# Threshold attention and a three-way max FFN: from two stages over DRAM to one fused, software-pipelined loop

## The chip, the cores and the metric

The kernel runs on one core of one Trainium2 chip. The metric is the device time of one execution, in microseconds; of several runs the median is taken.

## The reference

Sizes: 8 batches, 8 heads, 576 tokens, head width 64; q, k and v are fp32. The FFN has d_model 512 and d_ff 768 over 4608 tokens.

```python
scores = (q @ k.T) / sqrt(64)
thresh = max(scores, axis=-1) - tau                   # tau = 0.02
scores = where(scores >= thresh, scores, -1e9)
attn = exp(scores - max(scores)); attn = attn / (sum(attn) + 1e-9)
x = (attn @ v) laid out as 4608 x 512                 # heads side by side
h = maximum(maximum(x @ w1, x @ w2), x @ w3)          # 4608 x 768
out = h @ w_out                                       # fp32
```

Whether a score is kept depends on a difference of 0.02 from its row's maximum, and both kernels compute the scores in fp32; P, V, x and the weights are bf16.

## The kernel before

There are two stages, with x between them in DRAM (`xT`, 512 x 4608, bf16).

Attention loops over 64 heads. A head's 576 tokens are cut into five chunks, four of 128 and one of 64. For each chunk SyncE's queue loads v, q and k (lines 74 to 77, 32 KB each), VectorE casts v to bf16 (line 75), TensorE transposes q and k in one fp32 transpose (line 79) and VectorE copies the two halves out (lines 80, 81), both to partitions 0 to 63. Then, for each of five query chunks, two fp32 matmuls over 512 and 64 keys (line 89) with ScalarE copying the scaled scores out of PSUM (line 91), the row maximum and its negative on VectorE (lines 95, 97), Exp on ScalarE (line 99), one VectorE instruction that compares e with exp(-tau), multiplies, and sums the row (line 102), the reciprocal (108), and the division to bf16 `eall` (109). Last, for each key chunk, five bf16 transposes of P on TensorE (line 118), each copied out of PSUM by VectorE (line 120), and two matmuls with V as the stationary operand (lines 121, 124), accumulating the transposed output over key chunks; five casts and five stores to `xT` end the head (lines 130, 131).

The score tiles and the q/k transposes share a PSUM tag of two buffers ("sc"); the transposes of P have two of their own ("tr").

The FFN first loads the four weights (1536 KB each, fp32) and casts them on VectorE (lines 142, 147). Then 36 tiles of 128 tokens: a load of x, 24 matmuls of 384 columns (line 163, x stationary), a running maximum on VectorE (lines 167, 169), a cast (172), six transposes of h with copies (176, 177), six matmuls of 512 columns (180), a copy (183) and a store (184).

Waits and buffers are placed by the framework from the tiles' dependences, and it also orders each engine's instructions ahead of time, not strictly by the program: in the trace the next head's transposes of line 79 stand between this head's transposes of line 118. Within an engine the order is then fixed. Each DMA is issued by the engine named in the call: all of them by SyncE (SP in the profile).

## Time and profile before

| | before |
|---|---|
| runs | 2002.81, 2003.24, 2004.69 us; median 2003.24 |
| span of the profiled execution | 2002.6 us, its own time as far as it is recorded; 0.6 below the median |
| TensorE matmuls / weight loads | 80% / 36% of the span |
| VectorE, ScalarE | 67%, 23% |
| granted TensorE clock | 1.00 of full speed in every slice |
| DMA engines | q1 10.8% of 16 engines' span |

A share of busy time is an average over the two stages. The durations of TensorE instructions contain their latency, so what one more of a kind costs is read from the distance of starts, or from merged rows ("x7") that give the time of several in sequence. Idle time is put down to the instruction that ended last before the wait was over.

### The profile page before, as it was taken

The page shows a single profiled execution, that of the slowest core. Times are in us where ns is not written, and L with a number is a line of the kernel's source. Part 1 is how long each engine was busy: PE and PEld are TensorE (multiplying, and loading weights), DVE is VectorE, ACT ScalarE, POOL GpSimd, SP SyncE. Part 2 cuts the span into 40 slices and gives each one's busy share as a digit, 9 for nine tenths or more (in the row PEclk, how much of TensorE's full clock was granted, in tenths as well). Part 3 has the DMA queues.
Part 4 walks back from the last instruction along what each step waited for, and adds up shares of the span by engine and source line. Part 5 has one row for each costly group of instructions (what it writes and reads, how often), then busy time and mean ns, then how long its engine had stood idle before and what let it go on. Part 6 is the DMA issues. An engine that isn't in the chain of part 4 may idle for free.

```text
span 2002.6 us, 20193 instructions
## 1 busy us (share of the span) xinstructions
PE 1596.6 (80%) x5136; PEld 714.2 (36%) x5136; DVE 1349.6 (67%) x5308; ACT 461.1 (23%) x961; POOL 1.5 (0%) x10
## 2 busy tenths in 40 slices
PE   6777778877777877777787777788777778589998
PEld 3333333333333333333333333333333333244544
DVE  5666666666666666666666666666666666577777
ACT  2222222222222222222222222222222222100000
POOL 0000000000000000000000000000000000000000
PEclk9999999999999999999999999999999999999999
DMA  1000100000000000000000000000000000131121
GB/s 23 21 21 20 26 20 18 21 21 21 19 19 21 17 21 21 21 19 19 20 18 21 21 21 18 20 18 20 21 21 20 19 21 18 35 141 61 59 64 53
DMA packets 178227, 54.85 MB, mean 27 GB/s; under 512 B 171200, under 2 KB 171200, under 8 KB 178112
## 3 DMA queue, kind: packets, MB, share of 16 engines
q1 hardware_dynamic: 178112, 53.56, 10.8%
q8 instruction: 42, 0.69, 0.1%
q14 instruction: 73, 0.60, 0.1%
HBM read 39.32 MB, written 14.16 MB: 27 GB/s over the span
## 4 chain that ended last, share of the span: by engine, by line
PE 58%; DVE 26%; ACT 9%; issue 5%; DMA 1%; SPq 0%; ACTq 0%; DVEq 0%
PE ptile L89 28%; PE at L118 10%; DVE e L102 9%; PE optile L121 9%; ACT e L99 5%; DVE ats L120 5%; DVE mx L95 4%; ACT scores L91 4%; PE pt L163 4%; PE tp L79 3%; DVE eall L109 3%; PE op L180 3%; DVE hmax L169 2%; PE optile L124 2%; DVE hb L172 1%
## 5 line engine op out<-in xcount | busy, mean ns | idle before, releaser
L89 PE MATMUL ptile<-kT,qT 64*128 64x512 f32 (+3 forms) x1280 | 771.6, 746 | 70.0 <-ACT scores L91 69.9
L118 PE MATMUL at<-identb,eall 128*128 128x128 bf16 (+3 forms) x1600 | 371.9, 277 | 191.1 <-DVE ats L120 153.6
L91 ACT ACTIVATE scores<-ptile 128x512 f32<-128x512 f32 (+3 forms) x640 | 246.2, 405 | 1148.4 <-PE ptile L89 1148.0
L89 PEld LDWEIGHTS ptile<-kT,qT 64*128 64x128 f32 (+1 forms) x1280 | 341.4, 302 | 424.3 <-issue 206.7
L120 DVE COPY ats<-at 128x128 bf16<-128x128 bf16 (+3 forms) x1600 | 302.9, 211 | 252.9 <-PE at L118 224.2
L102 DVE SCALAR_TENSOR_TENSOR e<-e 128x576 f32<-128x576 f32 (+1 forms) x320 | 239.4, 748 | 281.5 <-ACT e L99 272.3
L118 PEld LDWEIGHTS <-eall 128*128 128x128 bf16 (+3 forms) x1600 | 164.9, 118 | 548.2 <-DVE eall L109 274.4
L99 ACT ACTIVATE e<-scores,nmx 128x576 f32<-128x576 f32 (+1 forms) x320 | 246.4, 771 | 120.7 <-DVE nmx L97 120.6
L95 DVE TENSOR_REDUCE mx<-scores 128x1 f32<-128x576 f32 (+1 forms) x320 | 237.8, 743 | 20.5 <-ACT scores L91 20.5
L121 PE MATMUL optile<-ats,vS 128*64 128x512 bf16 (+1 forms) x320 | 194.9, 609 | 68.6 <-DVE ats L120 68.0
L163 PE MATMUL pt<-t,xt 128*128 128x384 bf16 x864 | 178.8, 331 | 31.8 <-DVE t L142 18.0
L109 DVE TENSOR_SCALAR eall<-e,rs 128x576 bf16<-128x576 f32 (+1 forms) x320 | 161.9, 506 | 0.0
L79 PE MATMUL tp<-identf,vf 128*128 128x128 f32 (+1 forms) x320 | 123.4, 427 | 34.4 <-ACT scores L91 19.4
L163 PEld LDWEIGHTS <-xt 128*128 128x128 bf16 x864 | 85.2, 99 | 109.4 <-issue 56.9
L169 DVE TENSOR_TENSOR hmax<-hmax,pt 128x384 f32<-128x384 f32 x144 | 76.4, 551 | 34.8 <-PE pt L163 34.3
L81 DVE COPY kT<-tp 64x128 f32<-64x128 f32 (+1 forms) x320 | 89.4, 279 | 8.7
L80 DVE COPY qT<-tp 64x128 f32<-64x128 f32 (+1 forms) x320 | 84.2, 263 | 11.3 <-PE tp L79 4.3
L79 PEld LDWEIGHTS tp<-identf,vf 128*128 128x128 f32 (+1 forms) x320 | 56.4, 191 | 70.0 <-ACT scores L91 31.0
L124 PE MATMUL optile<-ats,vS 128*64 128x64 bf16 (+1 forms) x320 | 76.9, 240 | 3.7
L130 DVE CAST osb<-optile 64x128 bf16<-64x128 f32 (+1 forms) x320 | 73.4, 259 | 3.5 <-DMA xT<-osb 3.1
L121 PEld LDWEIGHTS <-vS 128*64 128x64 bf16 (+1 forms) x320 | 41.8, 131 | 64.7 <-issue 53.1
L180 PE MATMUL op<-wo,hT 128*128 128x512 bf16 x216 | 64.6, 381 | 0.0
(25 smaller groups left out, 413.0 us busy)
## 6 DMA issues: line engine op xcount, KB each, us to landing
out_dram<-osb SPq DMA_DIRECT2D x36, 256.0 KB, 2.0
vf<-in_v_dram SPq DMA_DIRECT2D x256, 32.0 KB, 1.7
vf<-in_q_dram SPq DMA_DIRECT2D x256, 32.0 KB, 1.8
vf<-in_k_dram SPq DMA_DIRECT2D x256, 32.0 KB, 1.8
xt<-xT SPq DMA_DIRECT2D x36, 128.0 KB, 2.2
tf<-in_moe_w_dram SPq DMA_DIRECT2D x3, 1536.0 KB, 9.8
xT<-osb SPq DMA_DIRECT2D x256, 16.0 KB, 1.7
wof<-in_moe_w_out_dram SPq DMA_DIRECT2D x1, 1536.0 KB, 16.7
```

Of the source, the lines that this page charges most:

```text
L79: nc.tensor.transpose(tp[:, :ck], vf[:ck, 1:].rearrange("p a d -> p (a d)"), identf[:ck, :ck])
L89: nc.tensor.matmul(ptile[:pm, :nn], qT[:, mo:mo + pm], kT[:, n0:n0 + nn], start=True, stop=True)
L91: nc.scalar.activation(out=scores[:pm, n0:n0 + nn], in_=ptile[:pm, :nn], func=Copy, scale=scale)
L95: nc.vector.reduce_max(mx[:pm], scores[:pm], axis=AX)
L99: nc.scalar.activation(out=e[:pm], in_=scores[:pm], func=Exp, bias=nmx[:pm], scale=1.0)
L102: nc.vector.scalar_tensor_tensor(out=e[:pm], in0=e[:pm], scalar=thr, in1=e[:pm], op0=AluOpType.is_ge, op1=AluOpType.mult, accum_out=sm[:pm])
L109: nc.vector.tensor_scalar_mul(eall[:pm, m], e[:pm], rs[:pm])
L118: nc.tensor.transpose(at[:ck, :pm], eall[:pm, m, co:co + ck], identb[:pm, :pm])
L120: nc.vector.tensor_copy(out=ats[:ck, m, :pm], in_=at[:ck, :pm])
L121: nc.tensor.matmul(optile[:, :4, :].rearrange("p a b -> p (a b)"), vS[:ck, c, :], ats[:ck, :4, :].rearrange("p a b -> p (a b)"), start=(c ...
L163: nc.tensor.matmul(pt, xt[:, kc, :], wt[:, kc, nb*384:nb*384+384], start=(kc == 0), stop=(kc == 3))
L180: nc.tensor.matmul(op, hT[:, c, :], wo[:, c, :], start=(c == 0), stop=(c == 5))
```

## The change

Nearly the whole body is replaced. What it does:

- One loop over 32 pairs of heads (four pairs a batch); the FFN of a batch is cut into 18 pieces (one that transposes X, 12 of hidden units, 5 of output rows), and one piece is put behind each unit of the attention of the next batch.
- q and k are loaded twice or in halves so that, after the fp32 transposes, q stands on partitions 0 to 63 and again on 64 to 127, and the first 288 keys on partitions 0 to 63, the other 288 on 64 to 127. A score tile is two matmuls of 288 columns, one on each half of the rows of the array, into two PSUM banks (`scores`).
- A pair has five units: units 0 to 3 take 128 queries of both heads, unit 4 the last 64 of both. The maximum is taken from PSUM directly. In units 0 to 2 ScalarE applies Prelu with slope 1e30 to score - max + tau: a score below the threshold becomes hugely negative, and the Exp that follows over both heads (1152 columns) makes it zero; no compare on VectorE. Units 3 and 4 take Exp and then the compare-and-multiply on VectorE.
- P is transposed by DMA transposes on SyncE's queue, one a unit, instead of on TensorE. P is padded with zeros to 640 keys.
- V has a 65th column of ones, so that the product with P also gives the row sums; P times V has P's transpose as stationary operand and 65 columns, and only its output is divided.
- The normalized output stays in SBUF (`X`), is transposed by DMA transposes, and the FFN computes h transposed, with the weights as stationary operand; there is no transpose of h, and ScalarE takes the first of the three products and the output copy.
- Weights and V are cast while they are loaded, by DMAs of GpSimd's queue, and the output is stored from that queue.
- P times V runs two units behind its P (`drain(2)`).

The diff, cut to its core; of the removed lines, which are all of the loops described above, four stand for the rest:

```diff
--- before
+++ after
...
-                for (n0, nn) in ((0, 512), (512, 64)):
...
-                nc.vector.tensor_scalar_mul(eall[:pm, m], e[:pm], rs[:pm])
...
-                    nc.tensor.transpose(at[:ck, :pm], eall[:pm, m, co:co + ck],
...
-            nc.tensor.transpose(pt, hb[:, c * 128:(c + 1) * 128], ident)
...
+STEEP = -1.0e30
...
+    wts = []
+    for i, w in enumerate((moe_w1, moe_w2, moe_w3)):
+        t = one.tile([128, 4, DF], BF16, name=f"w{i}")
+        for ko in range(4):
+            nc.gpsimd.dma_start(out=t[:, ko, :], in_=w[ko * 128:(ko + 1) * 128, :])
+        wts.append(t)
+    wo = one.tile([128, 6, DM], BF16, name="wo")
+    for ko in range(6):
+        nc.gpsimd.dma_start(out=wo[:, ko, :], in_=moe_w_out[ko * 128:(ko + 1) * 128, :])
+    NPB = 4
+    p_ring = [one.tile([128, 2, KP], BF16, name=f"pring{i}") for i in range(NPB)]
+    for t in p_ring:
+        nc.vector.memset(t[:, :, S:], 0.0)
+    NVB = 3
+    v_ring = [one.tile([128, 2, NK, D + 1], BF16, name=f"vring{i}") for i in range(NVB)]
...
+    ps_s = ctx.enter_context(tc.tile_pool(name="ps_s", bufs=2, space=PSUM))
+    ps_o = ctx.enter_context(tc.tile_pool(name="ps_o", bufs=1, space=PSUM))
+    ps_f = ctx.enter_context(tc.tile_pool(name="ps_f", bufs=2, space=PSUM))
+    def load(b, hp):
+        h0 = 2 * hp
+        qm = ld.tile([128, 2, 4, 2, D], F32, name="qm")
+        ql = ld.tile([128, 2, D], F32, name="ql")
+        kk = ld.tile([128, 2, 2, 2, D], F32, name="kk")
+        kl = ld.tile([32, 2, 2, D], F32, name="kl")
+        vt = v_ring[(b * NP + hp) % NVB]
+        for i in range(2):
+            h = h0 + i
+            for j in range(2):
+                nc.sync.dma_start(out=qm[:, i, :, j, :],
+                                  in_=q[b, h, 0:512, :].rearrange("(c p) d -> p c d", p=128))
+                nc.sync.dma_start(out=ql[i * 64:(i + 1) * 64, j, :], in_=q[b, h, 512:S, :])
                 nc.sync.dma_start(
+                    out=kk[:, i, :, j, :],
+                    in_=k[b, h, j * HS:j * HS + 256, :].rearrange("(c p) d -> p c d", p=128))
+            nc.sync.dma_start(
+                out=kl[:, i],
+                in_=k[b, h].rearrange("(j u) d -> u j d", j=2)[256:HS])
+            nc.gpsimd.dma_start(out=vt[:, i, 0:4, 0:D], in_=v[b, h, 0:512, :].rearrange("(c p) d -> p c d", p=128))
+            nc.gpsimd.dma_start(out=vt[0:64, i, 4, 0:D], in_=v[b, h, 512:S, :])
+        return dict(b=b, hp=hp, qm=qm, ql=ql, kk=kk, kl=kl, vt=vt)
+    def prep(L):
+        qt = qk.tile([128, 2, 512], F32, name="qt")
+        qtl = qk.tile([128, 128], F32, name="qtl")
+        kt = qk.tile([128, 2, HS], F32, name="kt")
+        for i in range(2):
+            tp = ps_f.tile([128, 512], F32, name="tp", tag="f")
+            for c in range(4):
+                nc.tensor.transpose(
+                    tp[:, c * 128:(c + 1) * 128],
+                    L["qm"][:, i, c].rearrange("p t d -> p (t d)"),
+                    identf)
+            nc.scalar.activation(out=qt[:, i], in_=tp, func=AF.Copy, scale=scale)
+            tk = ps_f.tile([128, 512], F32, name="tk", tag="f")
+            for c in range(2):
+                nc.tensor.transpose(tk[:, c * 128:(c + 1) * 128],
+                                    L["kk"][:, i, c].rearrange("p j d -> p (j d)"), identf)
+            nc.tensor.transpose(tk[:, 256:HS], L["kl"][:, i].rearrange("p j d -> p (j d)"), identf[:32, :32])
+            if i == 1:
+                nc.tensor.transpose(tk[:, 384:512], L["ql"].rearrange("p t d -> p (t d)"), identf)
+                nc.vector.tensor_scalar(out=qtl, in0=tk[:, 384:512], scalar1=scale, scalar2=None, op0=OP.mult)
+            nc.vector.tensor_copy(out=kt[:, i], in_=tk[:, :HS])
+        L.update(qt=qt, qtl=qtl, kt=kt)
+    def scores(L, i, c):
+        ps = ps_s.tile([128, 2, 512], F32, name="ps")
+        if c < 4:
+            for j in range(2):
+                r = slice(j * 64, (j + 1) * 64)
+                nc.tensor.matmul(ps[:, j, :HS], L["qt"][r, i, c * 128:(c + 1) * 128],
+                                 L["kt"][r, i, :], start=True, stop=True)
+        else:
+            for g in range(2):
+                for j in range(2):
+                    r = slice(j * 64, (j + 1) * 64)
+                    nc.tensor.matmul(ps[g * 64:(g + 1) * 64, j, :HS], L["qtl"][r, g * 64:(g + 1) * 64],
+                                     L["kt"][r, g, :], start=True, stop=True)
+        return ps
+    state = {"u": 0}
+    def unit(L, c):
+        n = 2 if c < 4 else 1
+        P = p_ring[state["u"] % NPB]
+        state["u"] += 1
+        masked = c >= 3
+        z = zz.tile([128, 2, S], F32, name="z")
+        for i in range(n):
+            ps = scores(L, i, c)
+            pv = ps[:, :, :HS]
+            nm = small.tile([128, 1], F32, name="nm")
+            nc.vector.tensor_reduce(out=nm, in_=pv, axis=mybir.AxisListType.XY, op=OP.max, negate=True)
+            zi = z[:, i].rearrange("p (j u) -> p j u", j=2)
+            if masked:
+                nc.scalar.activation(out=zi, in_=pv, func=AF.Exp, bias=nm)
+                nc.vector.scalar_tensor_tensor(out=P[:, i, :S], in0=z[:, i], scalar=thr, in1=z[:, i],
+                                               op0=OP.is_ge, op1=OP.mult)
+            else:
+                bm = small.tile([128, 1], F32, name="bm")
+                nc.vector.tensor_scalar_add(bm, nm, tau)
+                nc.scalar.activation(out=zi, in_=pv, func=AF.Prelu, bias=bm, alpha=-STEEP)
+        if not masked:
+            nc.scalar.activation(out=P[:, 0:n, :S], in_=z[:, 0:n], func=AF.Exp)
+        pt = pt_pool.tile([128, 2 * NK, 128], BF16, name="pt")
+        nc.sync.dma_start_transpose(out=pt[:, 0:n * NK, :], in_=P[:, 0:n].rearrange("p h k -> p (h k)"))
+        return pt
+    def pv_unit(L, c, pt):
+        if c == 0:
+            L["o"] = [ps_o.tile([128, 512], F32, name=f"o{i}") for i in range(2)]
+        for i in range(2):
+            o = L["o"][i] if c < 4 else L["o"][1]
+            if c < 4:
+                dst = o[:, c * 65:c * 65 + 65]
+                blk, cols = i * NK, slice(0, 128)
+            else:
+                dst = o[i * 64:(i + 1) * 64, 260:325]
+                blk, cols = 0, slice(i * 64, (i + 1) * 64)
+            for m in range(NK):
+                kr = 128 if m < 4 else 64
+                nc.tensor.matmul(dst, pt[:kr, blk + m, cols], L["vt"][:kr, i, m, :],
+                                 start=(m == 0), stop=(m == NK - 1))
+    def normalize(L, X):
...
+            nc.vector.reciprocal(rs[:, :n], ov[:, :, 64])
+            nc.vector.tensor_tensor(
+                out=X[:, 0:4, h * D:(h + 1) * D], in0=ov[:, 0:4, 0:64],
+                in1=rs[:, 0:4].unsqueeze(2).to_broadcast([128, 4, 64]), op=OP.mult)
...
+    def x_transposed(X):
+        xt = xp.tile([128, 5, 4, 128], BF16, name="xt")
+        for c in range(5):
+            r = 128 if c < 4 else 64
+            nc.sync.dma_start_transpose(out=xt[:, c, :, :r], in_=X[:r, c, :])
+        return xt
...
+        def hid(f, a):
+            c0, c1, r = (0, 2, 128) if a == 0 else (2, 5, 128)
+            hm = hp_.tile([128, 320], BF16, name="hm", bufs=3)
+            n = 256 if a == 0 else 320
+            dst = st["hT"][:, f, 0:256] if a == 0 else st["hT"][:, f, 256:S]
+            for wi in range(3):
+                pt = ps_f.tile([128, 512], F32, name="ph", tag="f")
                 for kc in range(4):
+                    w = wts[wi][:, kc, f * 128:(f + 1) * 128]
+                    if a == 0:
+                        nc.tensor.matmul(pt[:, 0:256], w, st["xt"][:, 0:2, kc, :], start=(kc == 0), stop=(kc == 3))
+                    else:
+                        nc.tensor.matmul(pt[:, 0:256], w, st["xt"][:, 2:4, kc, :], start=(kc == 0), stop=(kc == 3),
+                                         skip_group_check=True)
+                        nc.tensor.matmul(pt[:, 256:320], w, st["xt"][:, 4, kc, :64], start=False,
+                                         stop=(kc == 3), skip_group_check=True)
                 if wi == 0:
+                    nc.scalar.activation(out=hm[:, :n], in_=pt[:, :n], func=AF.Copy)
+                elif wi == 1:
+                    nc.vector.tensor_tensor(out=hm[:, :n], in0=pt[:, :n], in1=hm[:, :n], op=OP.max)
                 else:
+                    nc.vector.tensor_tensor(out=dst, in0=pt[:, :n], in1=hm[:, :n], op=OP.max)
+        for f in range(6):
+            for a in range(2):
+                pieces.append(lambda f=f, a=a: hid(f, a))
+        def outp(c):
+            r = 128 if c < 4 else 64
+            po = ps_f.tile([128, 512], F32, name="po", tag="f")
+            for f in range(6):
+                nc.tensor.matmul(po[:r, :], st["hT"][:, f, c * 128:c * 128 + r], wo[:, f, :],
+                                 start=(f == 0), stop=(f == 5))
+            ob = hp_.tile([128, DM], F32, name="ob", bufs=3)
+            nc.scalar.activation(out=ob[:r], in_=po[:r], func=AF.Copy)
+            nc.gpsimd.dma_start(out=out[b * S + c * 128:b * S + c * 128 + r, :], in_=ob[:r])
+        for c in range(5):
+            pieces.append(lambda c=c: outp(c))
+        return pieces
+    todo = []
+    pairs = [(b, hp) for b in range(B) for hp in range(NP)]
+    L = load(*pairs[0])
+    prep(L)
+    waiting = []
+    X = None
+    def drain(keep):
+        while len(waiting) > keep:
+            Lw, c, pt, Xw = waiting.pop(0)
+            pv_unit(Lw, c, pt)
+            if c == 4:
+                normalize(Lw, Xw)
+                if Lw["hp"] == NP - 1:
+                    todo.extend(ffn_pieces(Lw["b"], Xw))
+    for n, (b, hp) in enumerate(pairs):
+        if hp == 0:
+            X = xp.tile([128, 5, DM], BF16, name="X")
+        Ln = load(*pairs[n + 1]) if n + 1 < len(pairs) else None
+        for c in range(5):
+            pt = unit(L, c)
+            waiting.append((L, c, pt, X))
+            drain(2)
+            if todo:
+                todo.pop(0)()
+            if c == 2 and Ln is not None:
+                prep(Ln)
+        L = Ln
+    drain(0)
+    while todo:
+        todo.pop(0)()
```

## Rows read from the trace of the kernel before

**Rows 1.** The page: busy time and share of each engine, and the granted clock.

```profile
PE 1596.6 (80%) x5136; PEld 714.2 (36%) x5136; DVE 1349.6 (67%) x5308; ACT 461.1 (23%) x961; POOL 1.5 (0%) x10
...
PEclk9999999999999999999999999999999999999999
```

**Rows 2.** Busy time by stretch: one head, and most of the FFN.

```profile
core 0: us, PE busy (x) PEld busy (x) DVE busy (x) ACT busy (x) POOL busy (x), PEclk, DMA share, GB/s
1000.00:1027.05 27.05, 21.46 (x61) 9.31 (x60) 18.15 (x76) 7.19 (x16) 0.00 (x0) 1.00 0.09 19
...
1760.00:2002.60 242.60, 220.25 (x1287) 116.37 (x1284) 183.38 (x504) 0.00 (x0) 0.00 (x0) 1.00 0.21 65
```

**Rows 3.** The page: the chain that ended last, by engine and by line.

```profile
PE 58%; DVE 26%; ACT 9%; issue 5%; DMA 1%; SPq 0%; ACTq 0%; DVEq 0%
PE ptile L89 28%; PE at L118 10%; DVE e L102 9%; PE optile L121 9%; ACT e L99 5%; DVE ats L120 5%; DVE mx L95 4%; ACT scores L91 4%; PE pt L163 4%; PE tp L79 3%; DVE eall L109 3%; PE op L180 3%; DVE hmax L169 2%; PE optile L124 2%; DVE hb L172 1%
```

**Rows 4.** Timeline (start, duration, ..., idle before): the same ScalarE instruction, 26 heads apart.

```profile
1011.58 0.60 ACT L91 ACTIVATE scores<-ptile 128x512 f32<-128x512 f32 x1 [11.06 <-PE ptile L89]
...
1714.81 0.60 ACT L91 ACTIVATE scores<-ptile 128x512 f32<-128x512 f32 x1 [11.06 <-PE ptile L89]
```

**Rows 5.** Timeline of weight loads in the scores of one query chunk.

```profile
1015.86 0.50 PEld L89 LDWEIGHTS ptile<-kT,qT 64*128 64x128 f32 x2 [0.55 <-ACT scores L91]
1016.88 0.33 PEld L89 LDWEIGHTS ptile<-kT,qT 64*128 64x128 f32 x1 [0.52 <-ACT scores L91]
1017.73 0.34 PEld L89 LDWEIGHTS ptile<-kT,qT 64*128 64x128 f32 x1 [0.52 <-issue]
```

**Rows 6.** Timeline of TensorE: instructions of one kind in sequence.

```profile
1024.08 0.69 PE L79 MATMUL tp<-identf,vf 128*128 128x128 f32 x2 [0.30 <-ACT scores L91]
...
1901.83 1.13 PEld L163 LDWEIGHTS <-xt 128*128 128x128 bf16 x7
...
1906.13 0.26 PEld L176 LDWEIGHTS <-hb 128*128 128x128 bf16 x2
```

**Rows 7.** Groups by line and form: busy us, mean ns, idle before.

```profile
L99 ACT ACTIVATE e<-scores,nmx 128x576 f32<-128x576 f32 x256 | 196.8, 769 | 52.9 <-DVE nmx L97 52.9
L102 DVE SCALAR_TENSOR_TENSOR e<-e 128x576 f32<-128x576 f32 x256 | 191.4, 748 | 272.4 <-ACT e L99 272.3
L95 DVE TENSOR_REDUCE mx<-scores 128x1 f32<-128x576 f32 x256 | 190.8, 745 | 20.5 <-ACT scores L91 20.5
L91 ACT ACTIVATE scores<-ptile 128x512 f32<-128x512 f32 x256 | 152.8, 597 | 1081.5 <-PE ptile L89 1081.5
L79 PE MATMUL tp<-identf,vf 128*128 128x128 f32 x256 | 100.0, 442 | 32.3 <-ACT scores L91 19.4 <-DMA vf<-in_k_dram 6.2 <-DVE vS L75 0.8
L169 DVE TENSOR_TENSOR hmax<-hmax,pt 128x384 f32<-128x384 f32 x144 | 76.4, 551 | 34.8 <-PE pt L163 34.3 <-PE pt L176 0.5
L91 ACT ACTIVATE scores<-ptile 128x64 f32<-128x64 f32 x256 | 55.5, 217 | 23.6 <-PE ptile L89 23.3 <-PE at L118 0.3
L97 DVE TENSOR_SCALAR nmx<-mx 128x1 f32<-128x1 f32 x256 | 34.2, 134 | 0.1
L183 DVE COPY osb<-op 128x512 f32<-128x512 f32 x36 | 24.9, 692 | 19.8 <-PE op L180 19.8
L91 ACT ACT_TABLE_LOAD x1 | 1.3, 1283 | 0.7 <-PEq L201 0.7
```

**Rows 8.** Waits: who waited for whom, us in total, times, longest.

```profile
ACT scores L91 <- PE ptile L89: 1148.0, 382, 11.6
```

**Rows 9.** The page: DMA queue, and issues by line (KB each, median us to landing).

```profile
q1 hardware_dynamic: 178112, 53.56, 10.8%
...
vf<-in_v_dram SPq DMA_DIRECT2D x256, 32.0 KB, 1.7
...
tf<-in_moe_w_dram SPq DMA_DIRECT2D x3, 1536.0 KB, 9.8
xT<-osb SPq DMA_DIRECT2D x256, 16.0 KB, 1.7
```

**Rows 10.** Timeline of SyncE's queue: two issues in a row.

```profile
1000.04 0.43 SPq L76 DMA_DIRECT2D vf<-in_q_dram  x1
1000.51 0.43 SPq L77 DMA_DIRECT2D vf<-in_k_dram  x1
```

## The prediction

> **What bounds the kernel now.** The views were read in this order: busy shares, stretches, the chain, one head's timeline, durations by form, waits, transfers. TensorE is busy 80% of the span at a granted clock of 1.00, the 2.4 GHz level, in all forty slices, so no time is to be had from the clock [rows 1]. There are two stages. The attention of 64 heads takes 27.05 us a head: the same wait of ScalarE stands at 1011.58 and at 1714.81, 26 heads apart, and 703.23 / 26 = 27.05 [rows 4]. That is 1731 us. Weight loads and 36 token tiles of the FFN fill the rest up to 2002.6; its last 242.6 us show TensorE busy 220 us [rows 2]. In a head no engine is full: TensorE 21.5, VectorE 18.2, ScalarE 7.2 of 27.05 us [rows 2]. The chain changes hands, TensorE 58%, VectorE 26%, ScalarE 9% [rows 3], and ScalarE spends 1148 us waiting for scores [rows 8]. So two things hold attention: the fp32 score matmuls, and a relay between the engines that nothing else fills, because the FFN comes only afterwards.

> The price of a score column: each fp32 matmul is two instructions, and the weight loads around them start at 1016.88 and 1017.73, so a 512-column instruction takes 0.85 us, 1.66 ns a column [rows 5]. A head needs 5 x 576 columns twice, 9.6 us of its 27.

> **The change, by pair of heads (32 pairs).**

> *TensorE.* Scores: 20 matmuls of 288 columns, each two instructions of 288 x 1.66 = 0.478 us, 40 instructions, 19.1 us if one follows another. That is as many columns as before; the saving is only in overlap. The two key halves sit on partitions 0-63 and 64-127 and write different PSUM banks. In program order a unit has A A B B A A B B (A and B the halves); if an instruction may run beside its neighbour on the other half, eight slots become five, 2.39 us a unit, 12.0 us a pair. Bounds: 9.6 (all paired) and 19.1 (none). No row shows such an overlap, since before all K=64 operands lie on partitions 0-63; I take 12.0. Preparation: 15 fp32 transposes; two take 0.69 us where one takes 0.44, so 0.24 each [rows 6, 7], 3.6 us. P times V: 50 short matmuls (65 columns), each with its own 128-column weight load; two such loads take 0.26 us [rows 6], so 0.13 each, 6.5 us. The lower bound is their columns alone: seven 384-column steps take 1.13 us, 0.42 ns a column [rows 6], 0.03 each, 1.4 us. I take the load. FFN per batch: 72 weight blocks over 256 + 256 + 64 columns (0.107 + 0.107 + 0.10 with the load as floor of the short one), 22.6 us, and 30 steps of 512 columns at 0.215, 6.5 us; 29.1 a batch, 7.3 a pair. The 25 bf16 transposes a head and their VectorE copies go, as do the FFN's six transposes a tile. Sum: 12.0 + 3.6 + 6.5 + 7.3 = 29.4 us a pair, where the two stages before took 2 x 27.05 + 7.3 = 61.4.

> [...]

> *ScalarE.* A PSUM read costs 0.217 us at 64 columns and 0.597 at 512, so 0.163 + 0.00085 a column; Exp of 576 with a bias is 0.769 [rows 7]. Six Prelu at 0.65 to 0.77 (0.77 taken), three Exp of 1152 columns at 0.77 + 0.49 = 1.26, three masked Exp at 0.77, two Copies of 0.60, and a quarter of the FFN's copies (6 x 0.38 + 6 x 0.43 + 5 x 0.60 = 7.9): 13.9 us. The trace has one table load of 1.283 us and then Copy and Exp in turn with none [rows 7]; Prelu does not occur before. If each turn between Prelu and Exp needed a load, six a pair, ScalarE would have 21.6 us, still under TensorE. I take none.

> *VectorE.* Nine reductions at 0.745, six small adds at 0.134, three mask steps at 0.748 [rows 7]; PSUM reads by 0.551 at 384 and 0.692 at 512 [rows 7], so 0.13 + 0.0011 a column: two key copies at 0.45, the small query copy 0.27, normalization 1.5 (two products at 0.41, the rest small), a quarter of the FFN's 24 maxima (10.7) 2.7. Sum 15.1 us. Gone are the transpose copies, the divisions of whole rows, and the separate V casts. Both engines have about half of TensorE's load and lie beside it.

> *Transfers.* The loads become 2304 pieces of 256 bytes a head (q and k are read twice), 147,000 in all, plus weights and output, about the 178,112 packets that now take 10.8% of the engines [rows 9], so hidden. SP issues 14 loads a pair at 0.43 us [rows 10], 6 us. New are the crossbar transposes on the same queue: five a pair (45 blocks of 128x128, 320 KB an issue) and 160 blocks of X in all, 1600 blocks. No row shows one. The nearest by size is a weight load, 1536 KB in 9.8 us [rows 9]: 2.0 us an issue, 9 a pair. The nearest by destination, a small issue between SBUF and DRAM, lands in 1.7 us [rows 9]; were that the price of every block, an issue would take 17 us. I take 2 to 4 us. P times V runs two units behind its P, about 13 us at the rate below, so that is hidden; if it were not, SP would also hold up the next X transposes and loads queued behind.

> *New waits.* In units 0 to 2 ScalarE's first FFN copy stands behind the unit's Exp. After the last score come reduction 0.75, add 0.13, Prelu 0.77, Exp 1.26, copy 0.4, 3.3 us and about 0.5 of hand-offs. TensorE meanwhile has 1.3 us of P times V and two FFN groups, 1.3 us; its third group needs the copied PSUM buffer (two are shared), so it can stand 1.2 us, three units a pair; preparation shares the two buffers, perhaps another 1 us. Together 4.6 at most, 0 if the order of instructions lets scores go first; I take 3. What is late next is then TensorE itself.

> *Ends.* Start: P times V needs V, which on POOL's queue stands behind four weights of 1536 KB; at the 157 KB/us of [rows 9] that is 40 us, of which three units' scores cover half: 20 us. End: the last batch's X transposes, first FFN group and store, 12 us.

> **Sum.** 32 x (29.4 + 3.0) + 20 + 12 = 1069, say **1070 us**. The sum stands against the span of the profiled execution, 2002.6, which is 0.6 below the median 2003.24; nothing is added for that. Its own range, with stalls 0 to 4.6, P times V down to half, startup 10 to 40, and drains of about 1 us a pair: 920 to 1180.

> **The rivals.**

> A. The halves do not run at once. For it: nothing in the trace shows overlap, and fp32 takes two instructions in sequence. Then scores cost 19.1: 32 x (36.5 + 3) + 32 = 1296, say 1300 us. Against it: the operands lie on disjoint partitions and banks.

> B. The crossbar binds without passing the old time. From about 7 us an issue (32.4 / 4.5) the SP queue is later than TensorE; at 10 us, 1.0 a block, 1600 + 20 = 1620 us. Against it: the one DMA direction now used has 10.8% load.

> C. Slower: the same place, with every 128x128 block paying a landing of its own. At 1.7 us a block [rows 9], 1600 x 1.7 + 20 = 2740 us. It decides above 1.25 us a block (2003 / 1600). For it: a block is of the size at which landings now are all latency (16 and 32 KB alike in 1.7 [rows 9]). Against it: one instruction names ten blocks, and transfers before do overlap, issued 0.47 us apart and landing 1.7 us later [rows 9, 10]. [...]

> D. Table loads at each turn: 192 x 1.28 = 246 us on ScalarE; in the stall above it adds some 2 us in three units a pair, 1070 + 192 = 1260 us. Against it: Copy and Exp already share a table.

> E. Better packing (scores 9.6, P times V 1.4 to 3, no stall): 32 x 23.5 + 32, 780 to 900 us.

> **How the numbers follow.** The forecast 0.50, A 0.24, B 0.08, C 0.07, D 0.05, E 0.06. The range 920 to 1340 takes in the forecast, A and D; E, B and C are left out, 0.21. A measurement of this kernel can tell about 0.2%, 4 us, from no change. All cases but C are faster: 0.92; C is slower: 0.07; 0.01 for the point between.

> **What would show it.** Right: score instructions of the two halves start within 0.1 us of each other and a unit's eight fill about 2.4 us; TensorE leads the chain with over 60%; a crossbar issue lands within 4 us and P times V seldom waits for it; one ScalarE table load. Wrong: starts 0.48 us apart throughout (A); TensorE's longest wait is for the transposed P (B, C); a stretch with TensorE busy under 70% whose idle time ends in ScalarE or VectorE, which would mean that the relay, not a load, still sets the pace, and then even the four engine sums above are no guide.

## The result and the profile after

822.36 us (median of 4 runs, 817.67 to 827.43) against 2003.97 before: ratio 0.4104 [0.4087, 0.412]. The forecast was 1070, its range 920 to 1340; the time lies below both. The profiled execution has a span of 819.7 us. Here and below a ratio leaves out runs that took over 1.5% longer than the fastest of the same kernel; a median does not.

The page of the changed kernel: busy shares, granted clock, queue, crossbar issue (DMA_TRANSPOSE, median us to landing) and chain, against [rows 1, 3, 9].

```profile
PE 709.2 (87%) x5313; PEld 427.4 (52%) x5328; DVE 467.7 (57%) x1063; ACT 410.8 (50%) x585; POOL 116.6 (14%) x192
...
PEclk9977757998589987999679995899959997899979
...
q1 hardware_dynamic: 326912, 80.27, 53.3%
...
PE 40%; issue 25%; DMA 24%; DVE 4%; SPq 3%; ACT 2%; POOL 1%; POOLq 0%; ACTq 0%; DVEq 0%
...
pt<-pring SPq DMA_TRANSPOSE x160, 3.5
```

TensorE still leads the chain, with 40%, but it does its work in 709 us, where the forecast gave it 32 x 29.4 = 941. And the clock row, flat in [rows 1], now has dips. TensorE's waits, in us in total, times and longest:

```profile
PE o L193 <- DMA pt<-pring: 59.8, 44, 3.6
PE tp L118 <- DMA qm<-in_q_dram: 17.6, 3, 9.8
PE ph L242 <- DMA xt<-X: 9.3, 5, 4.5
PE o L193 <- DMA vring<-in_v_dram: 4.7, 6, 1.5
...
PE ph L242 <- ACT hm L249: 1.3, 6, 0.2
```

Groups by line and form of the changed kernel (against [rows 7]): the sizes taken for VectorE and ScalarE were right.

```profile
L164 DVE TENSOR_REDUCE nm<-ps 128x1 f32<-128x576 f32 x288 | 216.7, 754 | 120.8 <-PE ps L140 114.4 <-PE ps L146 3.8
L173 ACT ACTIVATE z<-ps,bm 128x576 f32<-128x576 f32 x192 | 141.9, 739 | 110.2 <-DVE bm L172 104.0 <-PE o L193 1.6
L175 ACT ACTIVATE pring<-z 128x1152 bf16<-128x1152 f32 x96 | 111.5, 1162 | 2.4
...
L122 ACT ACT_TABLE_LOAD x1 | 1.3, 1283 | 0.7 <-PEq L321 0.7
```

TensorE's timeline, same kernel: the second head's transposes, a unit's eight score instructions at three places, and a P times V that waits for its crossbar transpose.

```profile
22.16 1.09 PE L118 MATMUL tp<-identf,qm 128*128 128x128 f32 x4 [9.80 <-DMA qm<-in_q_dram]
...
25.55 2.29 PE L140 MATMUL ps<-kt,qt 64*128 64x288 f32 x8
...
395.38 1.07 PE L193 MATMUL o<-vring,pt 128*128 128x65 bf16 x10 [2.27 <-DMA pt<-pring]
...
399.55 2.55 PE L140 MATMUL ps<-kt,qt 64*128 64x288 f32 x8
...
424.39 1.24 PE L140 MATMUL ps<-kt,qt 64*128 64x288 f32 x8
```

The same eight take 2.29, 2.55 and 1.24 us. At 424.39 two instructions start together, the next two 0.34 us later and the two pairs after them 0.24 us apart, so the pairs do run at once; the rest of the factor is the clock, as the stretches around show (columns as in [rows 2]).

```profile
380.00:394.00 14.00, 11.16 (x81) 6.15 (x81) 7.66 (x15) 7.55 (x12) 1.10 (x2) 1.00 0.83 151
394.00:422.00 28.00, 25.39 (x123) 13.84 (x123) 11.11 (x27) 10.83 (x15) 2.64 (x4) 0.51 0.75 122
422.00:440.00 18.00, 16.69 (x155) 11.48 (x155) 12.50 (x30) 10.43 (x16) 2.62 (x4) 1.00 0.56 89
```

After the wait of 2.27 us the granted clock is 0.50 for 27 us, in which TensorE is busy over 90% of the time, and then 1.00 again. The levels 0.50 and 1.00 are called 1.2 and 2.4 GHz, an estimate that takes a column for a cycle: in this trace the FFN's 256-column products start 0.213 us apart at a recorded 0.50 and 0.109 at 1.00, 1.20 and 2.35 columns a ns. But at 25.55 the column reads 1.00 too, with the price of 1.2 GHz. That is the suspicion on which the experiments rest: until the first record of the clock in a trace, the column reads 1.00 whatever the engine has, and all durations of TensorE in the attention before were of 1.2 GHz.

### The profile page after: what moved, and what is told of

The parts are those of the page before. It is cut to its first block, busy times and chain, and to the rows that moved or that the text cites. A ratio compares the mean times of both kernels' runs of the same rounds, so it can differ in the third digit from the quotient of the medians.

```text
span 819.7 us, 14313 instructions
## 1 busy us (share of the span) xinstructions
PE 709.2 (87%) x5313; PEld 427.4 (52%) x5328; DVE 467.7 (57%) x1063; ACT 410.8 (50%) x585; POOL 116.6 (14%) x192
## 3 DMA queue, kind: packets, MB, share of 16 engines
q1 hardware_dynamic: 326912, 80.27, 53.3%
q0 software_dynamic: 44448, 17.31, 15.3%
## 4 chain that ended last, share of the span: by engine, by line
PE 40%; issue 25%; DMA 24%; DVE 4%; SPq 3%; ACT 2%; POOL 1%; POOLq 0%; ACTq 0%; DVEq 0%
DMA pt<-pring 15%; PE ps L140 11%; PE o L193 8%; PE ph L242 5%; PE tp L118 3%; PE po L263 3%; PE ps L146 3%; PE ph L244 3%; DMA kk<-in_k_dram 3%; DMA vring<-in_v_dram 3%; PE tk L125 2%; DMA xt<-X 2%; DVE nm L164 2%; DMA qm<-in_q_dram 1%; SPq L99 1%
## 5 line engine op out<-in xcount | busy, mean ns | idle before, releaser
L164 DVE TENSOR_REDUCE nm<-ps 128x1 f32<-128x576 f32 x288 | 216.7, 754 | 120.8 <-PE ps L140 114.4
L140 PE MATMUL ps<-kt,qt 64*128 64x288 f32 x1024 | 226.1, 502 | 5.2 <-ACT z L167 2.5
L173 ACT ACTIVATE z<-ps,bm 128x576 f32<-128x576 f32 x192 | 141.9, 739 | 110.2 <-DVE bm L172 104.0
L193 PE MATMUL o<-vring,pt 128*128 128x65 bf16 (+3 forms) x1600 | 140.2, 209 | 64.8 <-DMA pt<-pring 59.8
L193 PEld LDWEIGHTS <-pt 128*128 128x128 bf16 (+3 forms) x1600 | 98.1, 106 | 160.5 <-DMA pt<-pring 96.2
L140 PEld LDWEIGHTS ps<-kt,qt 64*128 64x128 f32 x1024 | 105.0, 211 | 60.1 <-issue 20.3
L175 ACT ACTIVATE pring<-z 128x1152 bf16<-128x1152 f32 x96 | 111.5, 1162 | 2.4
L244 PE MATMUL ph<-xt,w 128*128 128x256 bf16 x576 | 100.1, 287 | 1.1
L242 PE MATMUL ph<-xt,w 128*128 128x256 bf16 x576 | 89.6, 299 | 11.4 <-DMA xt<-X 9.3
L246 PE MATMUL ph<-xt,w 128*128 128x64 bf16 x576 | 91.4, 199 | 0.7 <-DMA xt<-X 0.7
L242 PEld LDWEIGHTS <-w 128*128 128x128 bf16 x576 | 55.8, 105 | 41.2 <-DMA xt<-X 14.2
L244 PEld LDWEIGHTS <-w 128*128 128x128 bf16 x576 | 59.0, 102 | 20.0 <-issue 9.1
L246 PEld LDWEIGHTS <-w 128*128 128x128 bf16 x576 | 58.2, 101 | 4.5 <-issue 2.4
L267 POOL DMA_DIRECT2D out_dram<-ob x40 | 22.5, 563 | 261.1 <-ACT ob L266 261.1
```

Source lines behind the costliest of these rows:

```text
L140: nc.tensor.matmul(ps[:, j, :HS], L["qt"][r, i, c * 128:(c + 1) * 128], L["kt"][r, i, :], start=True, stop=True)
L164: nc.vector.tensor_reduce(out=nm, in_=pv, axis=mybir.AxisListType.XY, op=OP.max, negate=True)
L173: nc.scalar.activation(out=zi, in_=pv, func=AF.Prelu, bias=bm, alpha=-STEEP)
L175: nc.scalar.activation(out=P[:, 0:n, :S], in_=z[:, 0:n], func=AF.Exp)
L193: nc.tensor.matmul(dst, pt[:kr, blk + m, cols], L["vt"][:kr, i, m, :], start=(m == 0), stop=(m == NK - 1))
L242: nc.tensor.matmul(pt[:, 0:256], w, st["xt"][:, 0:2, kc, :], start=(kc == 0), stop=(kc == 3))
```

## Experiments on the price

**x4_price**: TensorE alone, the whole computation left out: among others 40 fp32 products of 288 columns on one half of the rows, then 40 on the halves in turn, later pairs in turn with five short bf16 products. Each fp32 product is two instructions. The pauses of some 10 us between the blocks came out as 1.4 us, except the last.

> Only TensorE's prices, after gaps of some 10 us each: 24 fp32 matmuls of 512 columns on one half, 40 of 288 on one half, 40 of 288 on alternating halves, 80 bf16 of 512, 200 bf16 of 65 with a new weight load each, then 20 times a pair of halves and five short ones; nothing of the reference is computed. Theory 1: each fp32 instruction of 512 columns takes 0.85 us where the granted clock is 0.50 and 0.43 where it is 1.00; 288 on one half 0.24 at 1.00; on alternating halves half of that per instruction; short bf16 with its load 0.06 to 0.07 at 1.00, 0.10 at 0.50. Rival (fp32 costs four cycles a column at full clock, and the shorter tile or the second half is what made it cheap): 0.85 at 1.00 for 512 columns, and 0.48 for 288 on one half.

Measured, TensorE's timeline:

```profile
50.52 38.77 PE L70 MATMUL ps<-opb 64*128 64x288 f32 x80 [1.38 <-DVE J L52]
90.67 12.21 PE L76 MATMUL ps<-opc 64*128 64x288 f32 x80 [1.38 <-DVE J L52]
...
149.07 1.33 PE L94 MATMUL ps<-opf 64*128 64x288 f32 x4 [19.77 <-DVE J L52]
...
154.68 0.76 PE L94 MATMUL ps<-opf 64*128 64x288 f32 x4
155.36 0.33 PE L96 MATMUL ps<-opg 128*128 128x65 bf16 x5
155.62 0.76 PE L94 MATMUL ps<-opf 64*128 64x288 f32 x4
```

On one half an instruction cost 38.77 / 80 = 0.48 us, the price of [rows 5], though TensorE had no pause and the column read 1.00. On the halves in turn two start together, at a pitch of 0.48 us at first and 0.24 later in the same block. The change of pitch comes at 95.2 us, and there stands the first record of the clock in this trace, the beginning of a stretch of 1.00. After a pause of 19.8 us (recorded clock 0.50) four instructions take 1.33 us, then 0.76 at 1.00.

**x1_serial**: the changed kernel with both key halves on partitions 0 to 63.

```
-                nc.tensor.matmul(ps[:, j, :HS], L["qt"][r, i, ...], L["kt"][r, i, :], ...)
+                nc.tensor.matmul(ps[:, j, :HS], L["qt"][0:64, i, ...], L["kt"][:, i, j, :], ...)
```

> Both key halves stand on partitions 0-63, so no two score instructions can run at once; their number and columns are those of the changed kernel. Theory 1 (my prices of TensorE were read at its 1.2 GHz level, the row overlap is real): 40 instructions a pair cost 0.24 us each in sequence, 9.6 us, where paired they cost 4.8, so 4.8 us x 32 = 154 us more, with the stretches at half clock up to 200: 970 to 1020 us. Rival (the price per column of the prediction stands, five slots against eight of 0.478 us): 7.2 x 32 = 230 us more, 1050. Rival (the overlap is not what gained; the relay or the transfers set the pace): under 880.

948.91 us, ratio 0.4741 [0.472, 0.4763]: 126.6 us more than the changed kernel, 4.0 a pair, under what either theory gave. TensorE's timeline:

```profile
102.88 4.20 PE L141 MATMUL ps<-kt,qt 64*128 64x288 f32 x8
...
267.70 1.32 PE L141 MATMUL ps<-kt,qt 64*128 64x288 f32 x2
...
287.18 2.20 PE L141 MATMUL ps<-kt,qt 64*128 64x288 f32 x8
...
295.79 0.75 PE L141 MATMUL ps<-kt,qt 64*128 64x288 f32 x2
```

Eight take 2.20 one after the other where pairs take 1.24: the overlap is real, but at 2.4 GHz it saves 5 x 0.96 = 4.8 us a pair of heads. Two at 0.50 take 1.32 and at 1.00 0.75. The 126.6 us are not that price alone: the first record of the clock stands at 171.7 us in x1 (29.0 in the changed kernel), until then eight take 4.20, and TensorE waits 4.0 us for transposed P instead of 59.8.

**y3_before_rows**: the kernel before with row-tiled scores alone.

```
-                for (n0, nn) in ((0, 512), (512, 64)):
-                    ptile = ps_pool.tile([128, 512], F32, tag="sc")
-                    nc.tensor.matmul(ptile[:pm, :nn], qT[:, mo:mo + pm], kT[:, n0:n0 + nn], ...)
+                for j in range(2):
+                    r = slice(j * 64, j * 64 + 64)
+                    nc.tensor.matmul(pts[j][:pm, :288], qT[r, mo:mo + pm], kT[r, :], ...)
```

> The kernel before with row-tiled scores alone: q on both halves of the partitions, the 576 keys as two halves of 288, two PSUM tiles; softmax, transposes, PV and FFN as they were. Theory (pairs run at once, and the rows of the attention before stood at 1.2 GHz): a 288-column score instruction starts in pairs at a pitch of 0.24 to 0.28 us where the engine has risen to 2.4 GHz and at 0.48 where not; a head takes 18 to 22.5 us against 27.05, total 1430 to 1720. Rival (pairs run at once but the clock of the attention stays where it was): pitch 0.48, the scores of a head 9.6 to 4.8-6, head 22 to 23.5, total 1680 to 1780. Rival (the attention before is held by its relay through ScalarE and VectorE, not by scores): above 1850.

1882.08 us, ratio 0.9395 [0.9381, 0.9409]: the third case, the relay. Waits (us in total, times, longest):

```profile
ACT scores L98 <- PE ptile L95: 988.9, 448, 12.6
PEld L125 <- DVE eall L116: 341.4, 193, 2.6
PEld ptile L95 <- ACT scores L98: 240.5, 385, 1.3
```

ScalarE waits for scores (988.9 us, at most 12.6 at a time; [rows 8] had 1148.0), and within a head the weight loads of the scores wait for ScalarE's copy of the tile before (240.5 us); P times V still takes 609 ns for 512 columns. The halves do not start together there: of 1280 score instructions 3 start within 0.05 us of the one before, in the changed kernel 454 of 1024. So row-tiled scores alone are worth 6% here, and this run does not price the overlap.

**v1_before_fill**: the kernel before, with matmuls that nobody reads, 35 a head, to fill TensorE's pauses (and one buffer, not two, for the P times V sum).

```
+                    nc.tensor.matmul(fo[:, :], identb, fl, start=True, stop=True)
```

> The kernel before, with 35 more matmuls per head that nobody reads (bf16, 128x512, after each P transpose and two after each score unit; the PV accumulator has one buffer for that). Theory (1.2 GHz because TensorE has idle time): it rises to 2.4 GHz in the attention, PV's 512-column instruction falls from 609 to some 380 to 400 ns, the 512-column score from 0.85 to 0.43 us; the fillers cost 35 by 0.22 us = 7.7 us a head and the rest halves, so the time is 1650 to 2000. Rival (the prices of the attention are not the clock's): both prices stay, the fillers cost 35 by 0.43 = 15 us a head less the idle 5, time 2500 to 2800. Between: the one-half-row scores take the clock down again in each head, and prices are mixed.

1865.66 us, ratio 0.931 [0.9276, 0.9344]: with about 2200 matmuls more the kernel is 7% faster. The planner, which orders independent work freely, pulled the fillers forward, some 50 a head, until they ran out at 1030 us, so one run holds both cases. Its stretches, and the groups of each:

```profile
500.00:1000.00 500.00, 492.87 (x2306) 214.79 (x2350) 383.48 (x1582) 151.31 (x319) 0.00 (x0) 1.00 0.11 23
...
1100.00:1600.00 500.00, 393.95 (x1114) 170.82 (x1113) 335.65 (x1389) 131.88 (x275) 0.00 (x0) 0.50 0.09 19
...
L96 PE MATMUL ptile<-kT,qT 64*128 64x512 f32 x168 | 93.3, 636 | 0.0
L130 PE MATMUL optile<-ats,vS 128*64 128x512 bf16 x84 | 33.5, 398 | 1.0
...
L96 PE MATMUL ptile<-kT,qT 64*128 64x512 f32 x144 | 148.1, 1131 | 13.2 <-ACT scores L98 13.2
L130 PE MATMUL optile<-ats,vS 128*64 128x512 bf16 x76 | 46.3, 609 | 20.7 <-DVE ats L128 19.8
```

and the same two instructions in the kernel before, 512 columns of its FFN, and a stretch of its attention, where the column reads 1.00:

```profile
L89 PE MATMUL ptile<-kT,qT 64*128 64x512 f32 x512 | 526.6, 1131 | 46.8 <-ACT scores L91 46.8
L121 PE MATMUL optile<-ats,vS 128*64 128x512 bf16 x256 | 155.9, 609 | 68.6 <-DVE ats L120 68.0
L180 PE MATMUL op<-wo,hT 128*128 128x512 bf16 x216 | 64.6, 381 | 0.0
...
1100.00:1600.00 500.00, 395.17 (x1107) 171.30 (x1108) 336.94 (x1390) 133.62 (x278) 0.00 (x0) 1.00 0.09 20
```

This is the proof. With fillers a score instruction means 636 ns and P times V 398. Without them, 79% busy, the recorded clock is 0.50 and they take 1131 and 609, to the nanosecond what they take before, where TensorE is 79% busy as well and the column reads 1.00. The attention before ran at 1.2 GHz from end to end. The records of the clock agree: the column counts time without a record as 1.00, and the first record of the kernel before is a stretch of 1.00 from 1767.9 us, in the FFN, whose 384-column instructions start 0.32 us apart until then and 0.16 after. In the changed kernel and its twelve variants no score instruction before the first record takes under 681 ns; after it they fall to 402. Stores of a head's output (105 and 91 in 500 us, five a head) put a head at 23.8 us with fillers and 27.5 without.

**v2_rows_fill**: y3 with the same fillers.

> The kernel before with row-tiled scores alone (y3, 1882 us) and the same 35 fillers per head. Theory: it rises to 2.4 GHz, PV's 512-column instruction falls from 604 to 380 to 400 ns, a pair of 288-column scores from a pitch of 0.48 to 0.24 us, time 1550 to 1900, and below v1. Rival (prices not the clock's): 2400 to 2700.

1850.41 us, ratio 0.9234 [0.9177, 0.9292]. P times V takes 403 ns in 500 to 1000 us and 609 in 1100 to 1600, as in v1. The scores hold TensorE for 125 us of the first stretch, 155 in v1; that this brings little more would fit the relay that is left, and is not shown. The intervals of v1 and v2 overlap.

## Experiments on what the changed kernel still loses

For each kernel the table has the span, TensorE's waits for transposed P, the time recorded at half the clock (from windows of 1 us), and span less waits less half of that time, all in us. z3 has one unit between transpose and use, the changed kernel and z2 two, y2 four, the others three.

| kernel | span | waits | at half clock | rest |
|---|---|---|---|---|
| changed | 819.7 | 59.8 | 209.7 | 655.0 |
| z2_xspread | 817.0 | 60.9 | 205.9 | 653.2 |
| z3_lag1 | 894.1 | 98.1 | 278.2 | 656.9 |
| x2_lag3 | 741.6 | 28.8 | 109.6 | 658.0 |
| y1_lag3_spread | 735.7 | 28.1 | 113.6 | 650.8 |
| z1_lag3_xspread | 744.6 | 21.7 | 128.2 | 658.8 |
| y4_lag3_spread_ld3 | 750.9 | 31.9 | 126.5 | 655.8 |
| y2_lag4_spread | 757.4 | 24.3 | 143.9 | 661.2 |

The rest is the same within some 10 us: what separates these kernels is the waits and, more than these, the time at half the clock. Before its first record (29.0 us in the changed kernel, 17.2 in y1, 39.7 in y2, 49.2 in z1) each kernel runs at 1.2 GHz too, and the column does not count it: TensorE is busy 7.8, 6.6, 20.0 and 29.7 us there. With half of that, the rests lie between 644 and 653.

This is an accounting; the records say which wait stands before which low stretch. In the changed kernel 14 of the 15 recorded stretches at 0.50 begin during a wait for transposed P or at most 2.5 us after one, but most of the 44 waits are followed by none. In x1 six waits of 1.34 us for ScalarE are each followed by 30.7 to 41.0 us at 0.50, with TensorE busy throughout. The length of the wait does not set that of the stretch: in the changed kernel 2.31 us (at 187 us) were followed by 3.4 us at 0.50, and 2.27 us (at 393 us) by 27.3. What sets it stays open.

**x2_lag3**: `drain(2)` becomes `drain(3)`.

> P times V runs three units behind its P instead of two. Theory 2 (the wait for the transposed P is latency, about 2 us at most of the batches' ends, and each such wait is followed by some 27 us at a granted clock of 0.50): the wait of TensorE for pt falls from 60 us to under 15, the mean clock rises from 0.87 to over 0.95, and the time falls to 720 to 770 us. Rival (SyncE's queue or the DMA engines are short of throughput there, and more lag only moves the wait): 805 to 830 us and the same clock.

749.40 us, ratio 0.3733 [0.3717, 0.3748]: the time as expected, the rest not; waits 28.8 us (under 15 expected), clock 0.926 (over 0.95 expected).

**x3_nocross**: no transposes of P; P times V reads a constant tile.

> Leaves out the transposes of P: P times V reads a constant tile instead, everything else is issued. It prices the crossbar as a whole. Theory 2: 690 to 750 us, mean clock over 0.95, no wait for pt. Rival (TensorE's own load with other waits, those for X and the loads, sets clock and time): 790 to 825 us.

710.17 us, ratio 0.3534 [0.3504, 0.3565]; clock 0.969; packets of q1 137,472 for 326,912. The P transposes with their landing, the waits and the clock after them cost the changed kernel 112 us together. P times V does not wait for Exp and mask here either, so the crossbar's own part is at most that. By the accounting (43 us at half the clock) 683 us are left, some 27 above the table's rest; that was not taken apart.

**z3_lag1**: `drain(1)`.

> The changed kernel with one unit instead of two between a P transpose and its use, so TensorE waits in every unit. From the end of a unit's scores to its landed transposes about 7.2 us (0.75 + 0.74 + 1.16 + landing 3.5 + gaps); two units pass in that and the work between. Theory (waits take the clock down, and at 1.2 GHz every price is that of the rows before): eight score instructions at 2.3 to 2.6 us in most units, mean granted clock below 0.70, time 980 to 1100. Rival (the clock follows the busy share only loosely, or the waits alone count): the eight at 1.24 us, clock above 0.85, time 890 to 940.

895.72 us, ratio 0.4469 [0.446, 0.4478]: the rival's time. The waits rise and the clock falls (0.844), but 27 of its 28 stretches at 0.50 end within 21 us, so the theory's clock below 0.70 was too strong.

**y1_lag3_spread**: three units, and the FFN weights, loaded before everything till now, one per unit.

```
-            nc.gpsimd.dma_start(out=t[:, ko, :], in_=w[ko * 128:(ko + 1) * 128, :])
+            wq.append((t[:, ko, :], w[ko * 128:(ko + 1) * 128, :]))
```

> Three units between a P transpose and its use (as x2_lag3, 749.4 us), and the FFN weight loads, which the changed kernel issues before everything, are issued one per unit over the first 18 units. Theory (the first q and k wait behind the weights, TensorE's first work at 22 us): first TensorE work between 8 and 12 us, time 728 to 742. Rival (the start is bound by the loads of q and k themselves, and by the slow first units): no change against 749, 745 to 753. Rival (the spread loads stand in front of the transposes on SyncE's queue): above 753.

741.0 us, ratio 0.3668 [0.3653, 0.3684], the fastest version with the whole computation: 1.7% under x2 by the ratios, though its runs (732.35 to 747.65) reach into x2's (743.37 to 750.83). TensorE starts at 5.65 us, not 8 to 12 (7.39 in the changed kernel), and its first scores at 14.91 for 25.55, but then it waits for q again, and the recorded clock is 0.50 from 20.6 to 41.1 us.

**y2_lag4_spread**: y1 with four units, and five buffers for P and for its transpose instead of four.

> As y1_lag3_spread, with four units between transpose and use (P ring and transposed tiles five deep). Theory (the 29 to 39 us that TensorE still waits for transposed P at three units are landing time, and the stretches at half the clock follow these waits): waits for transposed P below 15 us, mean granted clock above 0.94, time 700 to 730. Rival (what is left of the wait is the queue of SyncE held by other instructions, not the landing): within 5 us of y1.

757.57 us, ratio 0.3783 [0.3778, 0.3789]: slower than y1, against both. Its waits are a little shorter, its recorded time at half the clock 30 us longer, and TensorE's busy time before the first record 13 us longer. Why is open.

**y4_lag3_spread_ld3**: y1 with three buffers for q, k and the rest of a load.

> As y1_lag3_spread, with three buffers instead of two for the loaded q, k and mask. Theory (the loads of the next pair wait on SyncE's queue for the transposes of the pair before, and P transposes stand behind them): the waits for transposed P fall by 5 to 15 us and the time by 5 to 20 us against y1. Rival (the queue is not what holds them): within 4 us of y1.

751.08 us, ratio 0.375 [0.3735, 0.3765]: above y1, outside both expectations; more of these buffers bring nothing.

**z1_lag3_xspread and z2_xspread**: the X transposes in pieces, and the hidden pieces in another order, in y1 and in the changed kernel.

> As y1_lag3_spread (741.0 us), with the five crossbar transposes of a batch's X, there issued one behind the other on SyncE (5.45 us for four, with the next P transposes behind them), spread over the first FFN pieces: two, then one at every other piece. Theory (what TensorE still waits for transposed P, 28 us in 25 waits, is the queue of SyncE held once per batch): waits below 12 us, less than 80 us at half the clock (113.6 there), time 700 to 725. Rival (the waits are the latency of Exp, mask and landing): within 5 us of 741. Rival (the start of a batch's first heads causes them, not the X transposes): waits 20 to 30 us, time 730 to 745.

> The changed kernel (two units between a P transpose and its use, 822 us) with the X transposes spread as in z1 alone. Theory (queue of SyncE): the 59.8 us of waits for transposed P fall to 25 to 40, the 210 us at half the clock to 130 to 170, time 765 to 795. Rival (two units are too short in every unit): waits above 50, time 805 to 830.

746.41 (0.3724 [0.3718, 0.3729]) and 822.47 us (0.4104 [0.4091, 0.4117]). SyncE's timeline of z1 shows why the test says nothing: the planner put them back together, four and one in most batches of z1. In z2 they stand as three and two, as they do in the changed kernel itself.

```profile
363.40 1.27 SPq L178 DMA_TRANSPOSE pt<-pring  x1
366.02 5.22 SPq L217 DMA_TRANSPOSE xt<-X  x4
371.35 1.36 SPq L178 DMA_TRANSPOSE pt<-pring  x1
```

**w1_loads_pool, w2_x_act, w3_both**: y1 with the q and k loads on GpSimd, the X transposes on ScalarE, and both.

> As y1_lag3_spread (741.0 us; waits for transposed P 28.1 us in 25, 113.6 us at half the clock), with the q and k loads issued by GpSimd instead of SyncE. Theory (loads that are issued back to back stand before the P transposes, 1 to 2 us each time): the waits fall below 12 us, the low stretches below 80 us, time 700 to 725. Rival (the loads hold nobody, P is late through Exp, mask and landing): within 5 us of 741. Rival (GpSimd's own queue, in which v loads wait for PV and stores for the output, now makes q and k late): waits of the q transposes above 30 us, time above 755.

> As y1_lag3_spread, with the five X transposes of a batch issued by ScalarE instead of SyncE (some 6.4 us of ScalarE per batch). Theory (they hold the P transposes behind them once per batch): waits 28.1 to 10 to 18 us, low stretches 113.6 to 60 to 90, time 710 to 730. Rival (not them): within 5 us of 741. Rival (ScalarE's Exp now stands behind them): above 748.

> Both: SyncE issues P transposes alone. Theory (its queue makes P late): waits below 6 us, low stretches below 60 us, time 680 to 710. Rival (latency of Exp, mask and landing): waits above 20 us, time 735 to 745.

772.33 (0.3845 [0.3828, 0.3861]), 800.59 (0.3986 [0.3972, 0.3999]) and 862.67 us (0.4287 [0.4262, 0.4313]): all slower. w1 has the time of its last rival and another cause: TensorE waits 9.5 us for q, but 65.4 for P, whose transposes now land after 4.5 us instead of 3.8, 14.0 at most (its profiled execution, 783.3 us, is 1.4% above the median), and the first record of the clock comes at 91.8 us, not 17.2. w2 goes as its last rival had it: TensorE waits 39.9 us for ScalarE's Prelu; besides, SyncE's P transposes wait for X's to land, 81.2 us in 14 waits. w3 has both waits (45.2 us for P, 45.6 for Prelu) and 32.3 us for ScalarE's copy of q besides, and loses more than the two together. What makes P late once per batch at three units stays open: none of the three queues could be relieved without loading another.

## Why the prediction was wrong

The failing step is the first price of its sum, that of a score column, 1.66 ns [rows 5], and with it 0.24 us a transpose and 0.13 a P times V product [rows 6, 7]. All are prices of 1.2 GHz; in the changed kernel a score slot of 288 columns mostly costs 0.24 us, not 0.48. The prediction read 1.00 in all slices [rows 1] and concluded that "no time is to be had from the clock". v1 and the first records of the clock show the opposite.

- **Overlap**: right. Pairs start together, in four slots and not five. That a unit's eight fill 2.29 us at 1.2 GHz, where 2.39 were forecast, is luck: it is four slots of 0.48 and latency. At 2.4 GHz the four slots are 0.24 each, 4.8 us a pair of heads instead of 12.0. Preparation is 15 x 0.13 = 2.0 instead of 3.6 (four transposes in 0.66 us), P times V 50 x 0.066 = 3.3 instead of 6.5 (ten in 0.80). FFN prices came from the FFN stage, which ran at 2.4 GHz, and held. 29.4 us becomes 17.4: 384 us too much over 32 pairs.
- **Stalls** of 3.0 us a pair by the FFN copy: not there. TensorE waits 1.3 us in all for that copy; the 96 us go.
- **Ends**: 22.16 us before the second head's transposes and, by the FFN of the last batch from 780 us, some 11 more than its share; 33 for 32. The size is luck at the start: TensorE waits 9.80 us for q there, not for V behind the weights.
- **Crossbar**: 3.5 us an issue, in the 2 to 4 taken; B and C fall by their times, though the sign named for them came: TensorE's longest wait in total is for transposed P. But "so that is hidden" was wrong once or more per batch: 59.8 us of waits, and about 105 us (half of 209.7) lost at half the clock.
- Put together: 1069 - 384 - 96 + 1 + 60 + 105 = 755; 65 us are left to 819.7, 2 us a pair. By an estimate from two pieces of the chain at full clock, shown below, some 45 of them lie at the turns between kinds: the eight score instructions take 1.17 us until the next kind starts, not 0.96, and the ten short products 0.73, not 0.66; 5 x 0.28 = 1.4 us a pair. The sum had the turns only in its range, as drains of about 1 us a pair. No run shows a drain; what the runs show in its place is this time until the next kind starts, and the bound from x4 below. The other 20 are of the size of TensorE's waits for X, V and ScalarE's z (9.3 + 4.7 + 4.9); they were not taken apart.
- **Rivals**: A falls with x1, D with the one table load. E named the time (780 to 900) by luck, with a wrong reason: better packing without stalls, at 1.2 GHz.
- **Transfers**: right. In x3, without the P transposes, the two queues move 137,472 + 44,448 = 181,920 packets, where about 178,000 were taken (k is read once; the count of 2304 pieces a head has it so). The P transposes add 326,912 - 137,472 = 189,440, which the count left out.

```profile
422.11 0.73 PE o L193 x10
...
428.39 1.17 PE ps L140 x8
```

In the changed kernel an issue of up to ten blocks lands in 3.5 us, and SyncE is busy 1.2 to 2.4 us with it; at C's 1.7 us for each of ten blocks it would be 17 us.

For a turn between half-row and full-row work x4 gives a bound: a block of four score instructions and five short products repeats every 0.94 us, of which 2 x 0.24 + 5 x 0.03 = 0.63 are its work by the blocks of one kind (200 short ones take 6.22 us), so a turn costs at most 0.16 us.

## What to carry to other kernels

Before a duration of TensorE goes into a sum, compare it with the same number of columns in another stretch, best one after a recorded change of the clock (here 609 ns in the attention, 381 in the FFN for 512 bf16 columns). Where durations of one shape differ by 1.5 to 1.8 (609 against 398, 1131 against 636) and starts by two (0.48 against 0.24), it was the clock here, whatever the column read. A stretch without pause is not enough to tell: x1 (from 40 us to 171.7) and x4 (38.77 us) have long ones at 1.2 GHz. A fused pipeline that keeps TensorE busy can then gain by the clock besides the work it removes, and a wait that is left can cost more than its length, through the clock after it (here 60 us of waits beside about 105 us lost at half the clock). After an edit to the order of issues, look at the queue's timeline for whether the planner kept it.
